# A tuned attention-then-FFN kernel: expert-by-expert FFN order, 1 MB weight loads, a new static order, and a joining copy that steps on its reading side

## Chip, core and metric

The kernel runs on one core of a Trainium2 chip. The metric is device time in microseconds (us), the median of several runs. Every run named here is of the fast state, with a mean granted TensorE clock of 1.00 unless said. A profile is one execution; its span is about 1.8 us shorter than the time. TensorE does the matmuls and transposes and writes them to PSUM, a buffer memory from which ScalarE and VectorE copy them; GpSimd does casts and copies; SyncE issues the transfers (DMA) in one queue. A transfer has landed when all its bytes are there.

## The reference, cut to what matters

```python
# q, k, v: (4, 8, 768, 64) float32; every row sees 8 global and the last 96 local keys
scores = q @ k.T / 8 - slope[h] * dist;  a = softmax(where(keep, scores, -1e9))
x = (a @ v).transpose(0, 2, 1, 3).reshape(3072, 512)
h = maximum(maximum(x @ w1, x @ w2), x @ w3)      # three "experts", 512 x 768 each
out = h @ w_out                                    # 768 x 512
```

The kernel works on 24 tiles of 128 tokens. A tile needs its own keys and those of the tile before it.

## The kernel before

Everything is issued in the order of one string, `SCHEDULE`. Each engine takes its own instructions from it first in, first out. Units are a letter and numbers:

```python
# l/L: load q or k (pair of tiles / one tile)   v: load v   w, o: load weights (all issued by SyncE)
# c/C, W, Q: cast to bf16 (last number: 0 ScalarE, 1 VectorE, 2 GpSimd)
# x/X: q/k transposed by TensorE and copied, X..4: by a DMA transpose;  T likewise for the attention output
# Sn.g: scores of tile n, group g (4 heads) + exp on ScalarE;   Mn.g: mask on VectorE
# (a last 1 in S: the bias is added by TensorE, and there is no mask)
# An.g: values matmuls + normalisation on VectorE;  G, V: copies of the global keys and values;  B, K: biases, masks
# Fc.f.j: FFN up, chunk c (2 or 4 tiles), block of 128 columns f, expert j;   Oc.t: FFN down, copy, store;  E: the last chunk's
SCHEDULE = """ ... S13.0.0 M13.0 L15 L16 v13 v14 S13.1.0 X14.4 F2.5.2 ... """
```

The parts that the change touches:

```python
def u_x(p, a, how):            # a pair of tiles was loaded with even and odd tokens side by side
    ...                        # 8 transposes into tp (PSUM, bf16): [c, e, j, i], e = even/odd
    copies[how % 2](pt[:, a].rearrange("c j (i e) -> c e j i", e=2), tp)      # stepped writes

def u_F1(c, f, j):             # 4 matmuls of 512 (or 256) columns into one of three PSUM buffers
    ...
    if j == 0:   nc.scalar.copy(h01, ps)
    elif j == 1: nc.vector.tensor_max(h01s[c, f], h01s[c, f], ps)
    else:        nc.vector.tensor_max(ht[c][:, f], h01s[c, f], ps)

def load_w(g, j):              # nine loads of 0.5 MB: 256 columns of one expert
    st = stage_pool.tile([128, 4, 256], FP32, name="wst", tag="wst")
    nc.sync.dma_start(out=st, in_=wsrc[j][:, g * 256:(g + 1) * 256].rearrange("(i p) f -> p i f", p=128))
```

The softmax here doesn't subtract the row's maximum and nothing guards it: scores larger than these inputs give would overflow.

## Time and profile before

| | kernel before |
|---|---|
| time, median of 3 | 183.83 us (183.54 to 184.5) |
| span of the profile | 181.9 us |
| TensorE busy | 167.0 us (92%) |
| first matmul / first FFN matmul | 5.69 / 26.27 us |
| last matmul's start to the end | 3.64 us |

The lines behind this table stand in the prediction. One caution: the profile of before lacks 22 of the program's 1528 matmul records. A missing record looks like a gap of two matmuls, 0.43 us from start to start. I count it as two matmuls, not as a wait.

### The profile page before, as it was taken

The page shows a single profiled execution, that of the slowest core. Times are in us where ns is not written, and L with a number is a line of the kernel's source. Part 1 is how long each engine was busy: PE and PEld are TensorE (multiplying, and loading weights), DVE is VectorE, ACT ScalarE, POOL GpSimd, SP SyncE. Part 2 cuts the span into 40 slices and gives each one's busy share as a digit, 9 for nine tenths or more (in the row PEclk, how much of TensorE's full clock was granted, in tenths as well). Part 3 has the DMA queues.
Part 4 walks back from the last instruction along what each step waited for, and adds up shares of the span by engine and source line. Part 5 has one row for each costly group of instructions (what it writes and reads, how often), then busy time and mean ns, then how long its engine had stood idle before and what let it go on. Part 6 is the DMA issues. An engine that isn't in the chain of part 4 may idle for free.

```text
span 181.9 us, 3991 instructions
## 1 busy us (share of the span) xinstructions
PE 167.0 (92%) x1506; PEld 94.3 (52%) x1528; DVE 123.4 (68%) x283; ACT 106.4 (58%) x165; POOL 31.6 (17%) x55
## 2 busy tenths in 40 slices
PE   0587999999999999997999999999999999999992
PEld 0353565567766687763455545445544545544441
DVE  3676477978987578867798758968456995264420
ACT  5968997947789596761437742326735536512222
POOL 6203424203303220212300040222022000000000
PEclk9999999999999999999999999999999999999999
DMA  5999999999998999999987998996799451610006
GB/s 147 271 252 274 294 305 310 306 246 296 267 236 167 226 256 228 261 207 216 193 184 147 272 208 167 241 177 131 200 315 193 90 119 29 231 58 0 4 9 221
DMA packets 93891, 36.18 MB, mean 199 GB/s; under 512 B 77104, under 2 KB 90160, under 8 KB 93872
## 3 DMA queue, kind: packets, MB, share of 16 engines
q1 hardware_dynamic: 93872, 35.92, 88.7%
q8 instruction: 12, 0.20, 0.5%
q14 instruction: 7, 0.06, 0.1%
HBM read 25.17 MB, written 6.29 MB: 173 GB/s over the span
## 4 chain that ended last, share of the span: by engine, by line
PE 71%; DMA 13%; SPq 4%; ACT 4%; DVE 3%; issue 2%; POOL 1%; DVEq 0%; POOLq 0%
PE h L336 41%; PE po L351 17%; DMA rawv<-in_v_dram 6%; PE sp L260 5%; DMA wst<-in_moe_w_dram 4%; SPq L156 3%; DMA rawp<-in_k_dram 3%; PE op L297 3%; PE op L300 2%; ACT P L265 2%; ACT qkT L221 1%; DVE qkT L221 1%; PE xtp L324 1%; PE tp L238 1%; PE tpp L218 1%
## 5 line engine op out<-in xcount | busy, mean ns | idle before, releaser
L336 PE MATMUL h<-xT,w 128*128 128x512 bf16 (+1 forms) x487 | 98.5, 348 | 0.8
L336 PEld LDWEIGHTS <-w 128*128 128x128 bf16 x504 | 47.0, 98 | 39.4
L265 ACT ACTIVATE P<-sp 128x1024 bf16<-128x1024 f32 (+1 forms) x48 | 43.8, 955 | 18.8 <-PE sp L260 18.7
L341 ACT CAST h<-h 128x512 bf16<-128x512 f32 (+1 forms) x42 | 22.1, 529 | 35.6 <-PE h L336 35.2
L343 DVE TENSOR_TENSOR h<-h,h 128x512 bf16<-128x512 bf16 (+1 forms) x42 | 25.5, 607 | 17.7 <-PE h L336 16.7
L351 PE MATMUL po<-wo,ht 128*128 128x512 bf16 (+1 forms) x145 | 33.2, 371 | 0.3
L284 DVE TENSOR_TENSOR P<-P,wmask 128x1024 bf16<-128x1024 bf16 x33 | 22.6, 690 | 11.8 <-ACT P L265 11.5
L345 DVE TENSOR_TENSOR ht<-h,h 128x512 bf16<-128x512 bf16 (+1 forms) x42 | 25.4, 608 | 3.0 <-PE h L336 0.2
L307 DVE TENSOR_TENSOR xb<-op,rz 128x256 bf16<-128x256 f32 x48 | 20.4, 424 | 1.6
L351 PEld LDWEIGHTS <-ht 128*128 128x128 bf16 x150 | 13.8, 98 | 14.2
L357 ACT COPY ost<-po 128x512 f32<-128x512 f32 (+1 forms) x22 | 12.6, 579 | 14.1 <-PE po L351 12.2
L260 PE MATMUL sp<-qkT 64*128 64x128 bf16 x352 | 15.4, 222 | 1.5 <-DVE qkT L221 1.0
L260 PEld LDWEIGHTS <-qkT 64*128 64x128 bf16 x352 | 10.1, 95 | 12.7 <-issue 8.5
L297 PEld LDWEIGHTS <-P 128*128 128x128 bf16 x192 | 13.1, 99 | 5.0 <-ACT P L265 1.7
L297 PE MATMUL op<-va,P 128*128 128x65 bf16 x160 | 13.2, 193 | 2.4 <-POOL va L176 1.1
L306 DVE RECIPROCAL rz<-op 128x4 f32<-128x4 f32 x48 | 8.5, 176 | 8.1 <-PE op L300 6.4
L300 PEld LDWEIGHTS <-P 128*128 128x128 bf16 x160 | 10.6, 97 | 2.9 <-issue 1.3
L218 PE MATMUL tpp<-identb,qkp 128*128 128x128 bf16 x64 | 6.2, 253 | 6.5 <-DVE qkp L170 6.5
L300 PE MATMUL op<-va,P 128*128 128x65 bf16 x128 | 10.6, 193 | 0.0
L400 POOL CAST w<-wst 128x1024 bf16<-128x1024 f32 x5 | 5.7, 1144 | 18.1 <-DMA wst<-in_moe_w_dram 15.0
L176 POOL CAST va<-rawv 128x512 bf16<-128x512 f32 x10 | 6.4, 640 | 12.8 <-DMA rawv<-in_v_dram 12.1
L218 PEld LDWEIGHTS <-qkp 128*128 128x128 bf16 x64 | 4.7, 114 | 6.8 <-DVE qkp L170 6.8
(67 smaller groups left out, 112.1 us busy)
## 6 DMA issues: line engine op xcount, KB each, us to landing
rawv<-in_v_dram SPq DMA_DIRECT2D x24, 256.0 KB, 5.3
out_dram<-ost SPq DMA_DIRECT2D x23, 256.0 KB, 2.9
wst<-in_moe_w_dram SPq DMA_DIRECT2D x9, 512.0 KB, 7.7
raw<-in_q_dram SPq DMA_DIRECT2D x16, 256.0 KB, 4.8
raw<-in_k_dram SPq DMA_DIRECT2D x16, 256.0 KB, 4.9
rawp<-in_q_dram SPq DMA_DIRECT2D x4, 512.0 KB, 6.4
rawp<-in_k_dram SPq DMA_DIRECT2D x4, 512.0 KB, 6.6
wst<-in_moe_w_out_dram SPq DMA_DIRECT2D x3, 512.0 KB, 6.2
```

The costliest lines, as they stand in the source:

```text
L218: nc.tensor.transpose(tp[:, e, jp], qb[p, a][:, e, 2 * jp:2 * jp + 2].rearrange("i h d -> i (h d)"), identb)
L260: nc.tensor.matmul(sp[:, hh, j2, ds], qT(T - ds, 1)[hsl, jp], qT(T, 0)[hsl, jp], start=not how, stop=True, skip_group_check=True)
L265: nc.scalar.activation(P[:, :, 0:n], sp.rearrange("p a b d n -> p (a b) d n")[:, :, 0:n], AF.Exp, bias=0.0, scale=scale)
L284: nc.vector.tensor_mul(P, P, wmask[:, g, :, 0:2])
L297: nc.tensor.matmul(o, P[:, i, 0], heads(va[T])[:, h], start=True, stop=(t == 0), skip_group_check=True)
L300: nc.tensor.matmul(o, P[:, i, 1], heads(va[T - 1])[:, h], start=False, stop=True, skip_group_check=True)
L307: nc.vector.tensor_tensor(out=x[:, 4 * g:4 * g + 4], in0=op[:, :, 0:64], in1=rz[:, :, None].to_broadcast([128, 4, D]), op=ALU.mult)
L336: nc.tensor.matmul(ps, w123[f // 2][:, dm, j, (f % 2) * 128:(f % 2) * 128 + 128], xT[c][:, dm], start=(dm == 0), stop=(dm == 3))
L341: nc.scalar.copy(h01, ps)
L343: nc.vector.tensor_max(h01s[c, f], h01s[c, f], ps)
L345: nc.vector.tensor_max(ht[c][:, f], h01s[c, f], ps)
L351: nc.tensor.matmul(po, ht[c][:, f, tt * 128:(tt + 1) * 128], wo[:, f, cols], start=(f == 0), stop=(f == NF - 1))
```

## The change

The intent: let the FFN start on fewer weights (expert after expert), move the last 512 columns of each expert in one 1 MB load, keep a tile's two score groups together, and make the joining copy cheaper. The core of the diff (the order is rewritten throughout, and with it which engine does a cast or a copy):

```diff
-        copies[how % 2](pt[:, a].rearrange("c j (i e) -> c e j i", e=2), tp)
+        copies[how % 2](pt[:, a].rearrange("c j (i e) -> c j i e", e=2), tp.rearrange("c e j i -> c j i e"))
 ...
-        st = stage_pool.tile([128, 4, 256], FP32, name="wst", tag="wst")
+        n = 256 * (1 + g)
+        st = stage_pool.tile([128, 4, n], FP32, name="wst", tag=f"wst{g}")
 ...
-    ... F0.0.0 M4.0 M4.1 A4.0 A4.1 F0.0.1 ... F0.0.2 F0.1.0 F0.1.1 w1.0 ...
+    ... F0.0.0 V3.1 F0.1.0 F0.0.1 w1.0 F0.1.1 A4.0 A4.1 F0.0.2 F0.1.2 ... F0.2.0 F0.3.0 F0.4.0 ...
 ...
-    ... S13.0.0 M13.0 L15 L16 v13 v14 S13.1.0 ...
+    ... L15 S11.0.0 M11.0 S11.1.0 v13 v14 v15 v16 M11.1 ...
```

More of the change, by code (lines that the diff above doesn't have):

```diff
@@ L25 @@
 SCHEDULE = """
-    B0.1 c0.0.1 B1.2 v0 l1.0 K0 l1.1 v1 K1 K2 B2.0 K3 K4 K5 B3.0 B4.0 B5.0 B6.0 c0.1.1 x0.0.1 x0.1.3
-    B7.0 K6 S0.0.1 c1.0.1 M0.0 S0.1.1 C0.1.2 K7 A0.0 c1.1.1 x1.0.2 M0.1 v2 A0.1 G0.1 S1.0.0 C1.1.0 T0.0
-    S1.1.1 M1.0 A1.0 l2.0 l2.1 M1.1 x1.1.1 G1.2 A1.1 c2.0.0 S2.0.1 M2.0 S2.1.1 M2.1 C2.1.2 v3 G2.0 V1.1
-    A2.0 x2.0.2 A2.1 V2.1 l3.0 c2.1.2 S3.0.1 M3.0 S3.1.1 T1.1 x2.1.0 w0.0 G3.1 C3.1.2 A3.0 c3.0.2 v4
-    M3.1 w0.1 x3.0.2 A3.1 W0.0.2 w0.2 T2.1 S4.0.1 v5 T3.1 C4.1.1 V3.1 l3.1 S4.1.1 W0.1.1 G4.0 F0.0.0
@@ L31 @@
-    M4.0 M4.1 A4.0 A4.1 F0.0.1 S5.0.0 S5.1.0 M5.0 T4.1 M5.1 c3.1.0 W0.2.2 F0.0.2 F0.1.0 F0.1.1 w1.0
-    W1.0.0 V4.2 C5.1.2 A5.0 A5.1 x3.1.0 F0.1.2 F0.2.0 w1.1 w1.2 W1.1.2 T5.1 W1.2.1 S6.0.0 S6.1.0 F0.2.1
-    M6.0 v6 w2.0 F1.0.0 F0.2.2 F0.3.0 F1.0.1 F1.0.2 F1.1.0 L8 M6.1 C6.1.1 F1.1.1 w2.1 G6.2 F0.3.1 W2.1.2
-    W2.0.0 A6.0 A6.1 F1.1.2 C8.0.0 F1.2.0 F0.3.2 S7.0.0 S7.1.0 v7 C7.1.2 v8 F1.2.1 M7.0 w2.2 F1.2.2
-    F1.3.0 o0 M7.1 F0.4.0 X8.3 F1.3.1 o2 A7.0 A7.1 W2.2.2 T6.0 F1.3.2 F1.4.0 C8.1.0 Q0.1 L9 Q2.1 F0.4.1
@@ L36 @@
-    V7.1 L10 G7.2 S8.0.0 S8.1.0 o1 C9.0.0 M8.0 M8.1 F0.4.2 v9 G8.0 F0.5.0 F0.5.1 A8.0 A8.1 v10 X9.0
-    C10.0.0 F1.4.1 Q1.2 F0.5.2 X10.4 T7.0 F1.4.2 S9.0.0 C9.1.0 L11 S9.1.0 T8.1 M9.0 F1.5.0 M9.1 v11 L12
-    O0.0.0 O0.1.0 O0.2.0 V8.1 A9.0 A9.1 T9.4 F1.5.1 C10.1.2 F1.5.2 G9.0 S10.0.0 S10.1.0 O0.3.0 C11.0.3
-    F2.0.0 X11.0 G10.0 C11.1.0 L13 M10.0 M10.1 V9.2 A10.0 v12 F2.0.1 A10.1 V10.1 T10.4 F2.0.2 F2.1.0
-    S11.0.0 S11.1.0 F2.1.1 F2.1.2 M11.0 M11.1 F2.2.0 F2.2.1 F2.2.2 F2.3.0 L14 C12.0.2 X12.0 A11.0 A11.1
@@ L41 @@
-    O1.0.0 S12.0.0 C13.0.1 M12.0 S12.1.0 M12.1 C12.1.2 O1.1.0 X13.0 A12.0 F2.3.1 F2.3.2 C14.0.2 A12.1
-    F2.4.0 F2.4.1 F2.4.2 T11.1 F2.5.0 F2.5.1 G12.1 S13.0.0 M13.0 L15 L16 v13 v14 S13.1.0 X14.4 F2.5.2
-    F3.0.0 F3.0.1 F3.0.2 F3.1.0 M13.1 F3.1.1 C15.0.1 C13.1.2 C14.1.2 C16.0.2 F3.1.2 A13.0 v15 L17 G13.2
-    A13.1 V13.1 X15.4 X16.4 F3.2.0 F3.2.1 F3.2.2 S14.0.0 S14.1.0 M14.0 M14.1 F3.3.0 v16 F3.3.1 F3.3.2
-    T12.4 C17.0.1 A14.0 A14.1 F3.4.0 F3.4.1 T13.4 T14.4 v17 F3.4.2 G14.2 S15.0.0 S15.1.0 M15.0 C15.1.1
@@ L46 @@
-    X17.4 O2.0.0 L18 G15.0 O2.1.0 M15.1 V14.2 A15.0 A15.1 F3.5.0 S16.0.0 v18 S16.1.0 T15.1 G16.1 L19
-    M16.0 F3.5.1 M16.1 V15.2 F3.5.2 C16.1.0 F4.0.0 A16.0 F4.0.1 F4.0.2 A16.1 O3.0.0 S17.0.0 T16.4
-    C18.0.2 M17.0 S17.1.0 V16.1 F4.1.0 C17.1.2 M17.1 F4.1.1 F4.1.2 F4.2.0 F4.2.1 C19.0.1 X18.4 C18.1.2
-    A17.0 A17.1 L20 L21 O3.1.1 X19.4 v19 C20.0.3 F4.2.2 S18.0.0 M18.0 v20 S18.1.0 M18.1 F4.3.0 F4.3.1
-    F4.3.2 F4.4.0 F4.4.1 F4.4.2 F4.5.0 A18.0 A18.1 C21.0.3 F4.5.1 X20.4 X21.4 F4.5.2 T17.4 G18.1 S19.0.0
@@ L51 @@
-    S19.1.0 G19.0 C19.1.2 M19.0 M19.1 T18.4 C20.1.2 O3.2.0 O3.3.0 A19.0 A19.1 T19.4 L22 O4.0.0 S20.0.0
-    M20.0 S20.1.0 O4.1.0 O4.2.0 M20.1 V19.2 A20.0 A20.1 L23 v21 G20.0 F5.0.0 F5.0.1 F5.0.2 F5.1.0 F5.1.1
-    F5.1.2 v22 T20.4 C22.0.3 V20.2 S21.0.0 M21.0 S21.1.0 M21.1 C21.1.1 F5.2.0 X22.4 G21.0 F5.2.1 F5.2.2
-    F5.3.0 A21.0 A21.1 V21.1 F5.3.1 F5.3.2 T21.4 C22.1.0 S22.0.0 S22.1.0 C23.0.3 M22.0 M22.1 F5.4.0
-    F5.4.1 F5.4.2 X23.4 A22.0 A22.1 v23 F5.5.0 G22.1 F5.5.1 F5.5.2 S23.0.0 T22.4 M23.0 V22.2 C23.1.0
@@ L56 @@
-    S23.1.0 M23.1 O4.3.1 O5.0.0 O5.1.0 A23.0 A23.1 O5.2.0 T23.0 O5.3.0 F6.0.0 F6.0.1 F6.0.2 F6.1.0
-    F6.1.1 F6.1.2 F6.2.0 F6.2.1 F6.2.2 F6.3.0 F6.3.1 F6.3.2 F6.4.0 F6.4.1 F6.4.2 F6.5.0 F6.5.1 F6.5.2 E
+    K0 K1 K2 K3 K4 K5 K6 K7 l1.0 v0 v1 B0.1 B1.0 c0.0.1 c0.1.1 B2.1 B3.1 B4.2 B5.0 B6.0 x0.0.2 x0.1.3
+    c1.0.0 S0.0.1 B7.2 S0.1.1 M0.0 M0.1 C0.1.2 C1.1.0 A0.0 G0.0 x1.0.2 A0.1 S1.0.1 S1.1.1 l1.1 M1.0 G1.1
+    l2.0 c1.1.2 l2.1 M1.1 c2.0.1 v2 w0.1 v3 v4 x1.1.2 w0.0 A1.0 A1.1 c2.1.2 V1.2 x2.0.1 C2.1.2 S2.0.1
@@ new lines @@
+    S2.1.1 G2.2 C3.1.2 T0.1 M2.0 M2.1 A2.0 x2.1.2 A2.1 V2.1 S3.0.1 S3.1.1 T1.0 T2.0 G3.2 W0.1.2 M3.0
+    M3.1 A3.0 W0.0.2 A3.1 S4.0.0 T3.1 w0.2 S4.1.0 M4.0 M4.1 G4.1 C4.1.1 W0.2.0 F0.0.0 V3.1 F0.1.0 F0.0.1
+    w1.0 F0.1.1 A4.0 A4.1 F0.0.2 F0.1.2 W2.0.0 S5.0.0 M5.0 l3.0 S5.1.0 M5.1 W1.0.2 F0.2.0 F0.3.0 F0.4.0
+    c3.0.2 x3.0.3 v5 C5.1.2 T4.0 w1.1 V4.2 A5.0 W2.1.0 l3.1 F0.5.0 W1.1.2 c3.1.1 F0.2.1 F0.3.1 x3.1.2
+    A5.1 F0.4.1 w1.2 W1.2.0 F0.5.1 S6.0.0 S6.1.0 v6 C6.1.0 v7 C7.1.0 T5.0 M6.0 M6.1 W2.2.2 F0.2.2 F0.3.2
@@ new lines @@
+    F0.4.2 F0.5.2 F1.0.0 F1.1.0 A6.0 F1.2.0 A6.1 L8 F1.0.1 F1.1.1 o2 Q2.0 G6.0 S7.0.0 o0 S7.1.0 F1.2.1
+    G7.0 F1.0.2 F1.1.2 T6.0 M7.0 M7.1 F1.3.0 F1.4.0 F1.5.0 A7.0 C8.0.2 X8.3 A7.1 Q0.0 v8 o1 L9 L10
+    F1.3.1 F1.4.1 F1.5.1 S8.0.0 S8.1.0 v9 V7.2 G8.1 L11 C8.1.0 M8.0 Q1.2 O0.0.0 v10 v11 C9.0.2 M8.1
+    O0.1.0 A8.0 X9.0 A8.1 V8.2 O0.2.0 C10.0.0 T7.1 F1.2.2 F1.3.2 F1.4.2 S9.0.0 M9.0 S9.1.0 M9.1 C9.1.2
+    L12 L13 L14 G9.1 X10.1 O0.3.0 F2.0.0 F2.0.1 A9.0 F2.1.0 A9.1 F1.5.2 F2.0.2 v12 F2.2.0 T8.1 S10.0.0
@@ new lines @@
+    S10.1.0 F2.1.1 F2.2.1 F2.3.0 C11.0.2 X11.0 M10.0 F2.4.0 M10.1 F2.1.2 F2.5.0 V9.2 G10.1 C10.1.2 A10.0
+    A10.1 V10.2 C11.1.2 C12.0.2 X12.4 C12.1.2 C13.0.0 X13.4 F2.2.2 T9.1 F2.3.1 F2.3.2 L15 S11.0.0 M11.0
+    S11.1.0 v13 v14 v15 v16 M11.1 O1.0.0 F2.4.1 A11.0 O1.1.0 T10.0 A11.1 F2.5.1 F2.4.2 T11.0 S12.0.0
+    M12.0 S12.1.0 G12.1 M12.1 F2.5.2 C14.0.0 F3.0.0 F3.1.0 A12.0 A12.1 F3.0.1 C15.0.1 X14.3 S13.0.0
+    S13.1.0 G13.1 M13.0 M13.1 X15.4 O2.0.0 C13.1.0 F3.0.2 C14.1.1 C15.1.2 F3.2.0 A13.0 A13.1 C16.1.1
@@ new lines @@
+    F3.1.1 F3.2.1 S14.0.0 S14.1.0 G14.2 V13.1 T12.4 M14.0 M14.1 F3.3.0 F3.1.2 F3.4.0 L16 T13.4 A14.0
+    A14.1 F3.3.1 F3.4.1 S15.0.0 S15.1.0 C16.0.3 L17 L18 M15.0 M15.1 F3.5.0 T14.4 O2.1.0 G15.2 V14.2
+    A15.0 X16.1 A15.1 V15.2 T15.4 F3.2.2 F3.3.2 C17.0.0 F3.4.2 S16.0.0 M16.0 S16.1.0 L19 F3.5.1 F3.5.2
+    X17.4 v17 A16.0 M16.1 F4.0.0 F4.1.0 C18.0.3 F4.0.1 F4.1.1 G16.2 v18 C17.1.0 A16.1 F4.0.2 X18.4
+    F4.1.2 S17.0.0 S17.1.0 L20 T16.4 F4.2.0 F4.3.0 F4.4.0 V16.1 C19.0.1 M17.0 X19.4 L21 M17.1 v19 A17.0
@@ new lines @@
+    A17.1 C20.0.3 v20 C18.1.1 O3.0.1 S18.0.0 M18.0 S18.1.0 O3.1.0 C19.1.2 M18.1 F4.2.1 A18.0 A18.1
+    F4.3.1 F4.4.1 G18.1 X20.4 S19.0.0 S19.1.0 C20.1.0 F4.5.0 M19.0 M19.1 T17.4 F4.2.2 O3.2.0 A19.0 A19.1
+    T18.4 F4.5.1 T19.4 L22 V19.2 G19.2 C21.0.3 O3.3.1 S20.0.0 M20.0 S20.1.0 G20.1 X21.4 v21 L23 v22
+    F4.3.2 v23 F4.4.2 A20.0 F4.5.2 M20.1 F5.0.0 F5.0.1 F5.1.0 A20.1 C22.0.1 C23.0.2 F5.0.2 F5.1.1
+    S21.0.0 S21.1.0 F5.2.0 M21.0 M21.1 F5.3.0 F5.2.1 F5.3.1 C21.1.0 C22.1.2 F5.1.2 X22.4 O4.0.0 V20.1
@@ L58 @@
+    A21.0 T20.4 A21.1 F5.2.2 F5.3.2 G21.0 S22.0.0 S22.1.0 M22.0 M22.1 F5.4.0 F5.4.1 X23.4 G22.1 C23.1.0
+    V21.2 A22.0 F5.5.0 A22.1 O4.1.0 F5.5.1 S23.0.0 M23.0 S23.1.0 F5.4.2 M23.1 T21.4 T22.4 O4.2.0 F5.5.2
+    O4.3.0 V22.1 A23.0 A23.1 T23.4 O5.0.0 O5.1.0 O5.2.0 O5.3.1 F6.0.0 F6.1.0 F6.2.0 F6.0.1 F6.1.1 F6.2.1
+    F6.3.0 F6.0.2 F6.1.2 F6.2.2 F6.4.0 F6.5.0 F6.3.1 F6.4.1 F6.3.2 F6.4.2 F6.5.1 F6.5.2 E
 """
@@ L109 @@
     xT_pool = ctx.enter_context(tc.tile_pool(name="xT", bufs=3))
-    stage_pool = ctx.enter_context(tc.tile_pool(name="stage", bufs=12))
+    stage_pool = ctx.enter_context(tc.tile_pool(name="stage", bufs=3))
     ht_pool = ctx.enter_context(tc.tile_pool(name="ht", bufs=2))
@@ L387, in load_w @@
     def load_w(g, j):
-        st = stage_pool.tile([128, 4, 256], FP32, name="wst", tag="wst")
+        n = 256 * (1 + g)
+        st = stage_pool.tile([128, 4, n], FP32, name="wst", tag=f"wst{g}")
         wst[g, j] = st
-        nc.sync.dma_start(out=st, in_=wsrc[j][:, g * 256:(g + 1) * 256].rearrange(
-            "(i p) f -> p i f", p=128))
+        nc.sync.dma_start(out=st, in_=wsrc[j][:, 256 * g:256 * g + n].rearrange("(i p) f -> p i f", p=128))
     def load_wo(i):
-        st = stage_pool.tile([128, 2, DM], FP32, name="wst", tag="wst")
+        st = stage_pool.tile([128, 2, DM], FP32, name="wost", tag="wost")
         wst["o", i] = st
@@ L399, in cast_w @@
     def cast_w(g, j, how):
-        copies[how](w123[g][:, :, j], wst[g, j])
+        src = wst[0, j] if g == 0 else wst[1, j][:, :, 256 * (g - 1):256 * g]
+        copies[how](w123[g][:, :, j], src)
     def cast_wo(i, how):
```

## The prediction

> **What bounds the kernel now.** I read the page first: its busy times, its 40 slices, its chain.
>
> ```profile
> PE 167.0 (92%) x1506; PEld 94.3 (52%) x1528; DVE 123.4 (68%) x283; ACT 106.4 (58%) x165; POOL 31.6 (17%) x55
> PE   0587999999999999997999999999999999999992
> DMA  5999999999998999999987998996799451610006
> PE 71%; DMA 13%; SPq 4%; ACT 4%; DVE 3%; issue 2%; POOL 1%; DVEq 0%; POOLq 0%
> ```
>
> The reader should see that TensorE is full from the seventh slice on, with one hole in the nineteenth, and that the transfers are full for the first 55 us. Matmul ends are modelled, so next I priced TensorE's work from start-to-start times: 0.216 us for a matmul of 512 columns, half of it for 256, 34 ns for a score matmul, 31 ns for one of 65 columns, 55 ns for a transpose. The counts by line then give: FFN up 360 x 0.216 + 144 x 0.108 = 93.4; FFN down 138 x 0.216 + 12 x 0.108 = 31.1; scores 352 x 0.034 = 12.1; bias 14 x 0.216 + 4 x 0.108 = 3.5; attention times values 352 x 0.031 = 10.9; transposes 152 x 0.055 = 8.4. Sum 159.4 us of the 181.9 us span. So 22.5 us are lost, and the rest of the reading is about where. The table of stretches and the timeline of TensorE answer that.
>
> ```profile
> 0.00:7.50 7.50, 1.03 (x8) 0.77 (x8) 2.93 (x16) 5.25 (x12) 3.42 (x13) 1.00 0.82 193
> 28.00:32.00 4.00, 3.95 (x42) 2.05 (x40) 3.00 (x7) 2.88 (x4) 1.77 (x3) 1.00 1.05 314
> 80.00:90.00 10.00, 8.79 (x68) 4.32 (x68) 7.64 (x15) 3.02 (x5) 2.79 (x5) 1.00 1.16 220
> 160.00:173.00 13.00, 12.95 (x61) 5.86 (x61) 6.92 (x11) 2.93 (x5) 0.00 (x0) 1.00 0.01 2
> 178.60:182.00 3.40, 0.00 (x0) 0.00 (x0) 0.42 (x1) 0.00 (x0) 0.00 (x0) 1.00 0.45 158
> ```
>
> ```profile
> 26.27 1.04 PE L336 MATMUL h<-xT,w 128*128 128x512 bf16 x3
> ```
>
> The second column is TensorE's busy time (matmuls). The first matmul starts at 5.69. The first FFN matmul is at 26.27, and of the 26.27 us before it only 11.7 us are priced work, a lag of 14.6 us. From 28 us on there is nearly none, except 1.5 us between 80 and 90, and a tail of 3.4 us (last copy and last store). So a change of order can win only in the first 28 us, at 85 us, or by making the tail shorter. The chain shows what the two holes wait for:
>
> ```profile
> 15.69 7.86 DMA wst<-in_moe_w_dram
> 23.61 1.05 POOL w L400
> ...
> 77.60 1.44 SPq L156
> 79.08 0.88 SPq L156
> 80.01 4.82 DMA rawv<-in_v_dram
> 84.97 0.78 POOL va L176
> 85.79 0.19 PE op L297
> ```
>
> At the start it is the arrival of the first FFN weights behind q, k and v in one queue; at 85 us it is one load of v, which stood in SyncE's order behind stores and q/k loads and was issued too late.
>
> **What the Trainium skill says.** (1) "TensorE: Matmul & The Clock Gate", section "Wait — 56ns, not 53.3ns?", gives N ÷ 2.4 GHz + 2.5 ns from start to start on a warm array: 215.7 ns for 512 columns, and twice that on a cold one. The trace agrees: 216 ns, and 427 ns at 13.6 us, before the clock is granted. No reordering makes the FFN matmuls faster. (2) "VectorE: DVE Perf Modes", section "What auto-detection actually checks": two elements per cycle need 16-bit tensors that all have step ±1. (3) "ScalarE: Activation LUTs", section "What ACT_TABLE_LOAD costs": 186 ns + 0.833 ns per element, so 1039 ns for 1024. (4) "PSUM — Partial Sum Buffer", section "Specifications (TRN2)": 8-byte cachelines, a non-contiguous pattern slows matmuls; of reads by ScalarE or VectorE it says nothing there, and no copy of this trace reads PSUM so. The rows for (2) and (3):
>
> ```profile
> L221 ACT COPY qkT<-tpp 128x1024 bf16<-128x1024 bf16 x5 | 6.5, 1320 | 0.2 <-PE tpp L218 0.2
> L243 ACT COPY qkT<-tp 128x1024 bf16<-128x1024 bf16 x4 | 4.1, 1025 | 0.5 <-PE tp L238 0.4
> L221 DVE COPY qkT<-tpp 128x1024 bf16<-128x1024 bf16 x3 | 3.8, 1300 | 0.0
> L325 DVE COPY xT<-xtp 128x512 bf16<-128x512 bf16 x8 | 3.4, 421 | 2.7 <-PE xtp L324 2.7
> ```
>
> L221 is the copy that joins even and odd tokens, here by stepped writes. ScalarE's plain copy of the same size takes the page's time (1025 against 1039), so stepped writing costs it 0.3 us. VectorE's 421 ns for 512 is two per cycle, the 1300 ns for 1024 one per cycle.
>
> **The change part by part.**
>
> *The joining copy.* Eight copies; the read is stepped now, the write plain. ScalarE should go back to about 1.05 us (five copies x 0.27 = 1.3 us of ScalarE). VectorE still has a stepped tensor, so I keep one per cycle, about 1.2 us. In the new order four of the first six copies lie on ScalarE, on the chain exp - copy - scores - exp that it is full with between 12 and 28 us.
>
> *Weights in 1 MB loads.* Nine loads become six; bytes stay. Rows become 2 KB: in this trace the output weights with 2 KB rows land 1.33 to 1.46 us apart per 0.5 MB, the others 1.42 to 1.60. At 0.1 us for each of six half-megabytes that is an estimated 0.6 us earlier at the end of the weights. Against this, one load lands as a whole: its first 256 columns can be used 1.5 us later than if they came alone.
>
> *FFN order.* With expert after expert, a weight load feeds two or four units of work before the next is needed. The number of matmuls does not change.
>
> *Mixture of the order.* The builds show 16 bias matmuls in place of 18 (-0.43) and 48 transposes of later q/k tiles in place of 40 (+0.44): TensorE's price is again 159.4.
>
> *The start, step by step.* I take landings from the trace: q/k pair loads 1.83 us apart, v 1.16, weights 1.5, and 2.97 for the first weight behind loads of other kind. In the new queue order: second load 6.8 (as now), three more pair loads and v0, v1 to 14.6, l2.1 16.4, v2 17.6, w0.1 20.5, v3 and v4 22.8, w0.0 24.3, w0.2 25.8, w1.0 28.8, then l3.0 and v5 31.7, w1.1 34.7, l3.1 36.5, w1.2 39.4. GpSimd's cast of 1.05 us makes w0.0 usable at 25.4. The other condition is the fourth tile's transposed output: ScalarE's masks and biases end at 8.65, then joining copy 1.05, cast 1.06, two short exps to 11.9, cast 0.6, copy to 13.7, and per tile two exps of 1.03 and a copy of 1.05; the fourth tile's exps end at about 22.7, its normalisation, transpose and copy at 24.5. So the first FFN matmul comes at about 25.4, with 10.8 us of priced work before it: a lag of 14.6 us, just as now. One unit (four matmuls of 512) is 0.86 us, and I walk on with lag 14.6: w1.0 needed at 31.7 and ready at 29.9; w1.1 needed at 36.0, ready at 35.8; w1.2 needed at 40.7, ready at 40.5. Two margins of 0.2 us with landings that I know to about 1 us: I charge 0.5 us.
>
> *The hole at 85 us.* The load that is waited for is the v of tile 13, which was requested between that tile's own two score groups. Now v13 to v16 are requested together at tile 11's scores. I expect this hole (1.2) and two small ones at 88 and 141 us (0.3 and 0.3) to go: -1.7.
>
> *Spacing of scores and values.* Both score groups side by side leave less other work between a tile's scores and its use: often 2.0 us before the first group, 2.8 before the second. The chain needs 1.03 + 0.69 + 0.1 = 1.9 and 1.03 more minus the second group's 0.28 = 2.6. It fits with 0.1 to 0.2 us; I charge 0.2 in all. The tail keeps its form: 0.
>
> Sum: -1.7 + 0.5 + 0.2 = -1.0, so 182.8.
>
> **Rivals.** (a) Stepped reading of PSUM is slow on ScalarE or VectorE, say 2 us a copy. For: the 8-byte cachelines and no example here. Against: one element per cycle already is the slow way on VectorE. The four copies then push the fourth tile by up to 4 us against 0.9 us of slack, and the time becomes about 185.5. (b) The first weight load does not pay the extra 1.5 us, or 2 KB rows are faster than estimated: weights are never waited for, the lag falls by 0.9, and with -1.7 it is about 181.2. (c) The 1 MB loads land as a whole and late, TensorE waits at 36 and 41 us about 1 us each: 183.9, no gain. (d) The loads of v were only the last of several things: a new wait behind SyncE's in-order stores takes the hole's place: about 184.
>
> **Range and chances.** Central 182.5, between the sum (182.8) and the friendlier (b). The pieces that can move are about 1 us each, so 8 in 10 lie in 180.7 to 184.7. Over 2% faster means under 180.2, which needs the lag of the start cut by 2 us besides: 0.08. Over 2% slower, above 187.5, needs (a) at its worst: 0.04. The rest 0.88.
>
> **What would show it.** Right: the hole in the nineteenth slice filled; first FFN matmul at 25 to 26 us with the weights' cast just before it; ScalarE's joining copy near 1.05 us, VectorE's near 1.2; TensorE's busy time unchanged within 1 us. Wrong: joining copies well over 1.3 us, first FFN matmul after 27, waits of TensorE on weights between 30 and 42 us longer than 1 us, a new wait on v or on a transpose by DMA after 60 us, or a first FFN matmul before 24.5, which would make it faster than I say.

## The result and the profile after

| | before | after |
|---|---|---|
| time, median | 184.0 us (4 runs) | 182.22 us (181.75 to 182.46, 4 runs) |
| the same, 5 more rounds | 183.94 us (11 runs) | 182.30 us (6 runs) |
| span of the profile | 181.9 us | 180.0 us; 180.7 in a second profile |
| first FFN matmul | 26.27 us | 24.98; 25.63 in the second |
| last weights of the FFN landed | 46.22 us | 39.05; 38.79 in the second |

The ratio is 0.990 (95% interval 0.9865 to 0.9934), and 0.9905 (0.9887 to 0.9923) in the five more rounds. A ratio is the mean time of one kernel's fast runs over that of the other's in the same rounds, so not quite the ratio of the medians.

The page of the changed kernel: busy times, TensorE's slices, the chain.

```profile
PE 167.2 (93%) x1534; PEld 94.5 (52%) x1534; DVE 122.0 (68%) x282; ACT 108.2 (60%) x164; POOL 35.0 (19%) x59
PE   0589979999999999999999999999999999999993
PE 78%; DMA 9%; SPq 9%; POOL 2%; issue 1%; DVE 0%; DVEq 0%; POOLq 0%
```

The hole in the nineteenth slice is filled, and TensorE's busy time has not moved. The timeline of TensorE alone, with the waits ahead of an instruction in brackets:

```profile
24.98 3.63 PE L336 MATMUL h<-xT,w 128*128 128x512 bf16 x16 [0.35 <-POOL w L402]
...
76.55 0.40 PE L260 MATMUL sp<-qkT 64*128 64x128 bf16 x8 [0.23 <-DMA qkT<-qkb]
...
101.55 3.63 PE L336 MATMUL h<-xT,w 128*128 128x512 bf16 x16 [0.45 <-DMA xT<-xb]
```

The first FFN matmul waits for the cast of its weights, as predicted. After 26 us only two waits are named, and both are new: on DMA transposes. The prediction had named such a wait as a sign of being wrong. The chain of waits at the start:

```profile
16.89 6.95 DMA wst<-in_moe_w_dram
23.89 1.05 POOL w L402
24.98 3.63 PE h L336 x16
```

In the kernel before this was not so, though the prediction reads it so. There the cast of the first weights is done 1.6 us ahead of the first FFN matmul (26.27):

```profile
23.61 1.04 POOL L400 CAST w<-wst 128x1024 bf16<-128x1024 f32 x1 [1.93 <-DMA wst<-in_moe_w_dram]
```

TensorE has no pause above 0.2 us there between 20.4 and 27.4 us. Its pauses lie before, around scores and values, and one of 0.4 us lies at 27.4, behind an exp that stands behind a joining copy on ScalarE.

The stretches with the second column as TensorE's busy time, for comparison with the rows in the prediction:

```profile
28.00:32.00 4.00, 4.00 (x47) 2.16 (x46) 3.45 (x8) 1.79 (x2) 2.19 (x3) 1.00 1.14 312
80.00:90.00 10.00, 10.00 (x100) 5.36 (x99) 9.06 (x22) 6.47 (x10) 0.83 (x2) 1.00 1.32 225
90.00:110.00 20.00, 19.55 (x175) 9.92 (x172) 16.61 (x35) 10.81 (x15) 2.76 (x6) 1.00 1.31 209
```

And the joining copy, one group for each engine:

```profile
L221 ACT COPY qkT<-tpp 128x1024 bf16<-128x1024 bf16 x5 | 5.0, 1009 | 1.5 <-PE tpp L218 1.5
L221 DVE COPY qkT<-tpp 128x1024 bf16<-128x1024 bf16 x3 | 3.7, 1220 | 1.2 <-PE tpp L218 1.2
```

ScalarE's copy fell from 1.32 to 1.01 us, VectorE's from 1.30 to 1.22.

To see where the time came from, I took each matmul's start-to-start time minus the prediction's price for it, and summed the rest by stretch. Missing records are put in by the order of the program, and the prices are scaled to the prediction's 159.4 us in all:

| TensorE's loss, us | before | after | after, second profile |
|---|---|---|---|
| up to the first matmul | 5.69 | 5.84 | 5.71 |
| first matmul to 30 us | 9.52 | 8.38 | 9.16 |
| 30 to 70 | 0.96 | 0.86 | 0.81 |
| 70 to 90 | 1.67 | 0.81 | 0.64 |
| 90 to 120 | 0.42 | 1.15 | 1.33 |
| 120 to the last matmul | 0.78 | 0.29 | 0.47 |
| last matmul's start to the end | 3.64 | 3.39 | 3.37 |

With the mean of the two profiles after: the first two rows -0.7, 30 to 70 us -0.1, 70 to 90 us -0.9, 90 to 120 us +0.8, the last stretch -0.4, tail -0.3. That makes about -1.6, near the measured -1.6 to -1.8. The two profiles after differ by 0.8 us in one row, so a part is known to some 0.4 us.

### The profile page after: what moved, and what is told of

It is laid out like the page before. It is cut to its first block, busy times and chain, and to the rows that moved or that the text cites. A ratio compares the mean times of both kernels' runs of the same rounds, so it can differ in the third digit from the quotient of the medians.

```text
span 180.0 us, 4007 instructions
## 1 busy us (share of the span) xinstructions
PE 167.2 (93%) x1534; PEld 94.5 (52%) x1534; DVE 122.0 (68%) x282; ACT 108.2 (60%) x164; POOL 35.0 (19%) x59
## 4 chain that ended last, share of the span: by engine, by line
PE 78%; DMA 9%; SPq 9%; POOL 2%; issue 1%; DVE 0%; DVEq 0%; POOLq 0%
PE h L336 50%; PE po L351 16%; PE sp L260 5%; SPq L163 4%; DMA wst<-in_moe_w_dram 4%; SPq L148 3%; DMA qkT<-qkb 3%; PE op L297 3%; DMA xT<-xb 2%; PE op L300 2%; PE tp L238 1%; SPq L392 1%; PE xtp L324 1%; POOL w L402 1%; POOL qkb L185 1%
## 5 line engine op out<-in xcount | busy, mean ns | idle before, releaser
L336 PE MATMUL h<-xT,w 128*128 128x512 bf16 (+1 forms) x504 | 101.4, 349 | 0.8 <-DMA xT<-xb 0.4
L336 PEld LDWEIGHTS <-w 128*128 128x128 bf16 x504 | 46.3, 98 | 40.5 <-POOL w L402 0.9
L351 PE MATMUL po<-wo,ht 128*128 128x512 bf16 (+1 forms) x150 | 33.9, 371 | 0.0
L284 DVE TENSOR_TENSOR P<-P,wmask 128x1024 bf16<-128x1024 bf16 x34 | 23.4, 693 | 9.0 <-ACT P L265 8.9
L357 ACT COPY ost<-po 128x512 f32<-128x512 f32 (+1 forms) x21 | 12.0, 577 | 18.4 <-PE po L351 16.0
L307 DVE TENSOR_TENSOR xb<-op,rz 128x256 bf16<-128x256 f32 x48 | 20.4, 424 | 1.7
L297 PEld LDWEIGHTS <-P 128*128 128x128 bf16 x192 | 13.7, 99 | 4.3 <-ACT P L265 1.2
L297 PE MATMUL op<-va,P 128*128 128x65 bf16 x160 | 14.0, 193 | 0.9 <-ACT P L265 0.8
L300 PEld LDWEIGHTS <-P 128*128 128x128 bf16 x160 | 10.8, 97 | 1.5
L300 PE MATMUL op<-va,P 128*128 128x65 bf16 x128 | 11.2, 193 | 0.0
L176 POOL CAST va<-rawv 128x512 bf16<-128x512 f32 x9 | 5.8, 644 | 17.2 <-PE h L336 9.4
L185 POOL CAST qkb<-raw 128x1024 bf16<-128x1024 f32 x5 | 5.2, 1038 | 19.1 <-issue 13.6
L202 POOL COPY va<-vaf 8x260 int32<-8x260 int32 x10 | 4.4, 440 | 22.5 <-PE op L300 22.5
```

The lines of the kernel that those rows point to most:

```text
L284: nc.vector.tensor_mul(P, P, wmask[:, g, :, 0:2])
L297: nc.tensor.matmul(o, P[:, i, 0], heads(va[T])[:, h], start=True, stop=(t == 0), skip_group_check=True)
L300: nc.tensor.matmul(o, P[:, i, 1], heads(va[T - 1])[:, h], start=False, stop=True, skip_group_check=True)
L307: nc.vector.tensor_tensor(out=x[:, 4 * g:4 * g + 4], in0=op[:, :, 0:64], in1=rz[:, :, None].to_broadcast([128, 4, D]), op=ALU.mult)
L336: nc.tensor.matmul(ps, w123[f // 2][:, dm, j, (f % 2) * 128:(f % 2) * 128 + 128], xT[c][:, dm], start=(dm == 0), stop=(dm == 3))
L351: nc.tensor.matmul(po, ht[c][:, f, tt * 128:(tt + 1) * 128], wo[:, f, cols], start=(f == 0), stop=(f == NF - 1))
```

## The experiments

All twelve passed the check against the reference. They ran in three groups; the median of before in them was 183.79, 183.94 and 183.89 us.

### The joining copy alone, on the kernel before

```diff
-        copies[how % 2](pt[:, a].rearrange("c j (i e) -> c e j i", e=2), tp)
+        copies[how % 2](pt[:, a].rearrange("c j (i e) -> c j i e", e=2), tp.rearrange("c e j i -> c j i e"))
```

> The kernel before with one part of the change: the joining copy reads its even and odd tokens stepped and writes plainly. My theory: ScalarE's copies fall from 1.32 to about 1.01 us and VectorE's from 1.30 to 1.22; before 26 us two of ScalarE's copies lie on the chain that sets the first FFN matmul, so it moves from 26.27 to about 25.7 and the time falls by 0.3 to 0.7 us, 183.3 to 183.7. Rival (the copy alone makes the whole gain of the start): minus 0.9 us or more. Rival (TensorE is back to back there anyway): no change.

Measured: 183.85 us, ratio 1.0009 (0.9992 to 1.0027). The expected gain did not come. The first FFN matmul did come earlier, at 25.80. In this profile TensorE then lost 1.3 us at 56 us. The chain of waits there:

```profile
48.96 6.34 DMA raw<-in_k_dram
...
55.38 0.29 ACT qkb L185
55.67 0.67 issue
56.33 0.59 ACT xT L325
56.92 0.04 issue
56.96 0.38 PE xtp L324 x4
```

A load of k landed at 55.30 (54.17 in the profile of before). ScalarE, first in first out, waited with a cast of it, and behind that cast stood the copy that frees the PSUM buffer which TensorE needs. So half a microsecond won at 26 us was lost in this profile to a load that is not any earlier.

### The same with that copy on another engine

```diff
-    ... X10.4 T7.0 F1.4.2 ...
+    ... X10.4 T7.1 F1.4.2 ...
```

> The kernel before with the stepped reading, and the copy of tile 7's transposed output on VectorE in place of ScalarE, where in the run with the stepped reading alone it stood behind a cast that waited for a late load and TensorE lost 1.3 us at 56 us. My theory (the copy's gain at the start was given back there): no hole at 56 us, ratio 0.997 to 0.999. Rival (TensorE gives the gain back elsewhere, or it is not there): ratio 1.000 or above.

Measured: 183.58 us, ratio 0.9984 (0.9967 to 1.0001). That is the expected size, but the interval touches 1, and the hole at 56 us did not close: 0.7 us of it stayed, now behind VectorE's queue. The same k load landed at 54.63 in this profile, and ScalarE's cast of it did not wait; so this run does not prove that the gain is given back there in every execution.

### v requested 29 entries earlier, on the kernel before

```diff
-    ... F2.3.0 L14 C12.0.2 ... L15 L16 v13 v14 S13.1.0 ...
+    ... F2.3.0 L14 v13 v14 C12.0.2 ... L15 L16 S13.1.0 ...
```

> The kernel before with the loads of v for tiles 13 and 14 requested right after the q and k of tile 14, some 20 us earlier; nothing else. My theory: the 1.2 us hole of TensorE at 85 us closes and nothing takes its place, minus 1.0 to 1.4 us, about 182.7. Rival (a new wait behind SyncE's in-order issues takes its place): within 0.3 us of the kernel before.

Measured: 183.05 us, ratio 0.996 (0.9939 to 0.9981), so -0.7 us, less than expected. The hole at 85 us is gone; a smaller one of 0.4 us shows at 88 us. The load was not issued some 20 us earlier but 6.7 (at 73.34 in place of 80.01): SyncE issued it right behind tile 14's k (72.72).

### Both together

```diff
 # the edits of the joining copy and of v13 v14 above, together
```

> The kernel before with the stepped reading and the early loads of v together. If the two are the gain and simply add, minus 1.4 to 2.0 us, as fast as the changed kernel (182.2). If the order of the FFN, the weight loads or the new order of the start carry part of it, it stays 0.5 us or more behind the changed kernel.

Measured: 182.51 us, ratio 0.9933 (0.9904 to 0.9962). Between the two expectations. With v mended the joining copy seems to bring something (0.996 to 0.9933), and some 0.3% seems left to the changed kernel (0.9905). The intervals overlap, so neither step is shown; by the middle values they are about 0.5 us each. In this profile the k load landed at 53.99, there is no hole at 56 us, and the first FFN matmul is at 26.09.

### The changed kernel with the old joining copy

```diff
-        copies[how % 2](pt[:, a].rearrange("c j (i e) -> c j i e", e=2), tp.rearrange("c e j i -> c j i e"))
+        copies[how % 2](pt[:, a].rearrange("c j (i e) -> c e j i", e=2), tp)
```

> The changed kernel with the old joining copy, stepped writing. My theory: the first FFN matmul waits for the cast of its weights, which ends at 24.94, only 0.2 us after the transposed output of the fourth tile; three of ScalarE's copies of 0.3 us each lie on the way to that output, so it comes about 0.6 us later and the time rises by 0.4 to 0.9 us, 182.6 to 183.1. Rival (the weights hide it): no change, 182.2. Rival (the copy carries the whole start): plus 1 us or more.

Measured: 182.39 us, ratio 0.9929 (0.9911 to 0.9948), against 0.9905 (0.9887 to 0.9923) for the changed kernel in other rounds: +0.24%, about 0.4 us. The intervals overlap, so this is not shown, and the reason I gave did not hold. TensorE's timeline:

```profile
25.46 3.63 PE L336 MATMUL h<-xT,w 128*128 128x512 bf16 x15 [0.77 <-POOL w L402]
```

The first FFN matmul still waits for the cast, and comes between the 24.98 and 25.63 of the changed kernel's two profiles. So in this order the weights hide the joining copy at the start. In the kernel before they do not: the three profiles with the stepped reading have the first FFN matmul at 25.80, 25.87 and 26.09, the others at 26.25, 26.27 and 26.75, and the pause at 27.4 us is gone in the three.

### The changed kernel again

```diff
 # no edit
```

> The changed kernel itself, unaltered, in the same rounds as the three next. All theories: its ratio to the kernel before stays at 0.990 (0.9865 to 0.9934); its trace shows the first FFN matmul at 25.0 and two holes of TensorE at about 76 and 101 us of 0.3 to 0.7 us, if these are of the order and not of chance.

Measured: 182.30 us, ratio 0.9905. The first FFN matmul is at 25.63, not at 25.0: it moves with the landing of its weights (24.48 in place of 23.83). The hole at 101 us is there again (0.66 us), so it belongs to the order. The one at 76 us is not in this profile, but it is in the next one (0.64 us).

### The changed kernel with v requested late

```diff
-    ... S11.1.0 v13 v14 v15 v16 M11.1 ... S13.0.0 S13.1.0 ...
+    ... S11.1.0 M11.1 ... S13.0.0 v13 v14 v15 v16 S13.1.0 ...
```

> The changed kernel with the loads of v for tiles 13 to 16 requested where the kernel before has those of 13 and 14, between tile 13's two score groups. My theory (the request's place makes the hole): a hole before tile 13's values of 1 to 2 us comes back and the time rises by 0.9 to 2 us. Rival (the hole of the kernel before came from its stores and loads ahead in SyncE's order, which this order does not have there): no hole, no change.

Measured: 182.30 us, ratio 0.9904 (0.9884 to 0.9925). No change, and no hole before tile 13's values. My theory, and the prediction's reason, fell: it is not the unit at which v is requested. SyncE's issues in the two kernels, in the timeline of its queue (start, duration, what), first before and then this run:

```profile
75.92 0.39 SPq L156 DMA_DIRECT2D raw<-in_q_dram  x1
76.37 1.18 SPq L156 DMA_DIRECT2D raw<-in_k_dram  x1
77.60 1.44 SPq L156 DMA_DIRECT2D raw<-in_q_dram  x1
79.08 0.88 SPq L156 DMA_DIRECT2D raw<-in_k_dram  x1
80.01 2.09 SPq L163 DMA_DIRECT2D rawv<-in_v_dram  x2
```

```profile
76.98 1.33 SPq L358 DMA_DIRECT2D out_dram<-ost  x2
78.36 4.30 SPq L163 DMA_DIRECT2D rawv<-in_v_dram  x4
```

In the kernel before, v stands behind the q and k loads of two tiles that are not needed until later. Here only two stores are ahead of it: v of tile 13 lands at 83.06 in place of 84.82, and tile 13's values begin at 84.98 without a wait. The edit moved less than it seems to: the unaltered changed kernel, which requests this load two tiles earlier, issues it at 76.25, only 2.1 us before this run.

### Four entries exchanged in the kernel before

```diff
-    ... S13.0.0 M13.0 L15 L16 v13 v14 S13.1.0 ...
+    ... S13.0.0 M13.0 v13 v14 L15 L16 S13.1.0 ...
```

> The kernel before with four entries of its order exchanged: the loads of v for tiles 13 and 14 stand in front of the q and k loads of tiles 15 and 16 and not behind them. My theory after the last runs (the hole came from standing behind four loads in SyncE's order, not from being requested at tile 13): v of tile 13 is issued at about 76 in place of 80.0 and lands about 81, the hole at 85 us is gone, and the time falls as with the loads 20 us earlier, by 0.5 to 1.2 us, ratio 0.994 to 0.997. Rival (it must be requested a tile or more ahead): a hole of 0.5 us or more stays and the time falls by less than 0.3 us.

Measured: 182.91 us, ratio 0.9949 (0.9925 to 0.9972), about -0.9 us, as much as asking farther ahead within the noise. v of tile 13 was issued at 76.23 and landed at 80.27. The stretch from 70 to 90 us, TensorE's busy time in the second column, first before and then this run:

```profile
70.00:90.00 20.00, 18.69 (x185) 11.55 (x186) 15.36 (x36) 9.40 (x15) 4.44 (x7) 1.00 1.15 228
```

```profile
70.00:90.00 20.00, 20.00 (x195) 12.27 (x193) 15.50 (x38) 10.43 (x17) 4.62 (x7) 1.00 1.19 223
```

Closing this hole is the largest single part of the change's gain, and an exchange of two pairs of loads is enough for it.

### The 1 MB loads as two halves each

```diff
-        nc.sync.dma_start(out=st, in_=wsrc[j][:, 256 * g:256 * g + n].rearrange("(i p) f -> p i f", p=128))
+        for gg in ((0,), (1, 2))[g]:       # a tile and a load of 256 columns each
+            nc.sync.dma_start(out=st, in_=wsrc[j][:, 256 * gg:256 * gg + 256].rearrange("(i p) f -> p i f", p=128))
```

> The changed kernel with each 1 MB load of weights made as two loads of 0.5 MB of 256 columns, one after the other in the same place of the queue. My theory: the loads are not what the gain rests on; the second half lands within 0.3 us of where the 1 MB load lands and the time is within 0.3 us of the changed kernel. Rival (rows of 2 KB are worth it): the weights end 0.6 us later and TensorE waits for them, plus 0.5 us. Rival (the halves come earlier, which helps): minus 0.3 us.

Measured: 182.54 us, ratio 0.9927 (0.9904 to 0.995), against 0.9905 (0.9887 to 0.9923) in the same rounds. The intervals overlap, so a cost is not settled. My expectation of the landings was wrong: the last half landed at 40.54, the 1 MB load at 38.79 in the same rounds. The rows of 2 KB are worth about what the prediction estimated: the 1 MB loads follow the load ahead of them by 2.73 to 2.81 us, 1.4 per 0.5 MB, four of the six halves by 1.50 to 1.57, so some 0.7 us in all (estimated from these). The rest comes from one half that landed 2.28 us after the one ahead of it, at 35.47, and from the k load behind it; I have no reason for that. TensorE did not wait for these weights; the profile has one extra gap of 0.26 us at 38 us, ahead of the transposes of a k load that lands 1.5 us later too.

### The old FFN order in chunks 2 to 6, in the same slots

```diff
-    ... F4.0.0 F4.1.0 ... F4.0.1 F4.1.1 A16.1 F4.0.2 F4.1.2 ...
+    ... F4.0.0 F4.0.1 ... F4.0.2 F4.1.0 A16.1 F4.1.1 F4.1.2 ...      # so in every chunk from 2 on
```

> The changed kernel with the FFN of its chunks 2 to 6 in the old order, the three experts of one block of columns after another, in the same slots. My theory: TensorE has no wait there in either order, so within 0.3 us of the changed kernel. Rival (runs of the same expert keep ScalarE and VectorE from taking turns, and the order is part of the gain): plus 0.5 us or more, seen as holes before FFN matmuls after 60 us.

Measured: 187.75 us, ratio 1.0198 (1.0176 to 1.022). Slower than both kernels, far outside my theory; the rival has the direction. The largest loss is a gap of 3.2 us from one matmul's start to the next, at 111.55 us. The timeline of this kernel there (start, busy time, what; the bracket is idle time before it):

```profile
109.05 1.94 ACT L265 ACTIVATE P<-sp 128x1024 bf16<-128x1024 f32 x2 [0.25 <-PE sp L260]
...
110.87 0.59 ACT L341 CAST h<-h 128x512 bf16<-128x512 f32 x1
111.50 0.69 DVE L343 TENSOR_TENSOR h<-h,h 128x512 bf16<-128x512 bf16 x1 [2.09 <-ACT h L341]
112.29 0.69 DVE L345 TENSOR_TENSOR ht<-h,h 128x512 bf16<-128x512 bf16 x1
...
113.41 0.67 DVE L185 CAST qkb<-raw 128x1024 bf16<-128x1024 f32 x1
114.01 1.28 DVE L284 TENSOR_TENSOR P<-P,wmask 128x1024 bf16<-128x1024 bf16 x2
```

A first expert's matmuls fall right behind a tile's scores. Their copy waits on ScalarE behind two exps of about 1 us. VectorE idles for 2.1 us because its next instruction, the second expert's maximum, needs that copy, and the two masks stand behind it. So the values matmuls wait until 114.74. The pause also cost clock (0.50 from 115 to 118 us). The stretch of 100 to 120 us, in which the last but two columns are the granted clock, the transfers' share and GB/s:

```profile
100.00:120.00 20.00, 17.08 (x130) 8.02 (x131) 13.98 (x29) 7.72 (x11) 0.82 (x2) 0.91 0.93 167
```

Values matmuls after it run 50 to 60 ns apart in place of 30. This does not say that the expert order is better as such: the kernel before runs the old order without such holes, in slots that were laid for it. It says that FFN order and slots are one thing.

### The old FFN order in the first chunk

```diff
-    ... F0.2.0 F0.3.0 F0.4.0 ... F0.5.0 F0.2.1 F0.3.1 ...
+    ... F0.2.0 W1.1.2 F0.2.1 W1.2.2 F0.2.2 ... F0.3.0 F0.3.1 F0.3.2 ...
```

> The changed kernel with the FFN of the first chunk, from its third block of columns on, in the old order, all three experts of a block before the next block; the order of the loads in the queue is kept, the casts of the weights are placed before their first use. My theory (expert after expert is what makes the 1 MB loads usable, since a load feeds four units of 0.86 us): TensorE waits at about 32 us for the second expert's load (cast ends 35.6) and at 36 for the third's (cast ends 40.1), together 5 to 7 us, time 187 to 189. Rival (the order of the FFN does not matter at the start because the transfers are the bound in any order): within 1 us.

Measured: 191.67 us, ratio 1.0413 (1.0382 to 1.0443). The direction and the waits are as expected, the cost is above what I gave (187 to 189). TensorE's timeline:

```profile
35.44 1.04 PE L336 MATMUL h<-xT,w 128*128 128x512 bf16 x4 [2.53 <-POOL w L402]
39.94 1.89 PE L336 MATMUL h<-xT,w 128*128 128x512 bf16 x4 [3.46 <-POOL w L402]
```

The two waits are where the landings put them (35.6 and 40.1 expected). From 28 to 42 us the granted clock was 0.84, and the four matmuls after the second pause took 1.89 us in place of 1.04; that part I had not counted. (The edit also moves the casts of the weights and puts the load requests together, in the same order.) With loads of one expert's 512 columns, a block cannot be finished before three loads have landed; expert after expert each load feeds four units.

### A mend of the two new holes

```diff
-    ... V10.2 C11.1.2 C12.0.2 X12.4 ... A15.1 V15.2 T15.4 ...
+    ... C12.0.2 X12.4 V10.2 C11.1.2 ... A15.1 V15.2 T15.1 ...
```

> The changed kernel with its two new holes mended: tile 15's output transposed by TensorE (copy on VectorE) in place of a DMA transpose that TensorE waited for at 101 us; tile 12's q/k cast put in front of two other operations on GpSimd, so that its DMA transpose starts about 1 us earlier. My theory: the 0.6 us hole at 101 us goes for 0.22 us of transposes, the one at 76 us goes where it showed; 0.3 to 0.8 us faster than the changed kernel, ratio to before about 0.987. Rival (the earlier TensorE only waits for the next thing): no change, 0.990.

Measured: 182.89 us, ratio 0.9944 (0.9929 to 0.996), slower than the changed kernel. The mend failed. TensorE's timeline:

```profile
96.76 0.27 PE L324 MATMUL xtp<-identb,xb 128*128 128x128 bf16 x2 [0.64 <-DVE qkT L243]
97.31 0.28 PE L324 MATMUL xtp<-identb,xb 128*128 128x128 bf16 x2 [0.28 <-DVE xb L307]
```

I put the transposes where the DMA transpose was issued, right behind the tile's values. A DMA waits there beside TensorE; TensorE's own transposes wait in its queue, first for a PSUM buffer and then for the normalisation, 1.2 us in all. The hole at 101 us closed and a larger one opened at 97. There is no hole at 76 us in this profile, but that one comes and goes. Two FFN units later would be the place to try; that was not run. No run here beats the changed kernel.

## Why the prediction was right, point by point

**The time.** 182.5 us predicted, 182.2 to 182.3 measured, inside 180.7 to 184.7, and neither 2% faster nor 2% slower, to which it gave 0.88. Part of that is luck: the charge for weights (0.5) did not come and the start and the tail brought 0.9 that was not counted, while the waits after 90 us cost 0.6 more than charged and the holes gave 0.4 less. The price of TensorE's work has two slips: with the printed prices FFN up is 93.3 and the scores 12.0, so 159.1 in all; nothing hangs on it.

**What bounds the kernel.** Held: busy time 167.0 and 167.2, and nearly all that was won or lost lies in the first 28 us, at 85 us, in new waits and a little in the tail.

**The joining copy.** Its duration held: 1.05 and 1.2 us predicted, 1.01 and 1.22 measured. Rival (a), slow stepped reads of PSUM, is out. What it is worth in time is not shown: in the new order it is off the path at the start, and on the kernel before alone it brought nothing clear of noise.

**The start.** First FFN matmul predicted at 25.4 behind the weights' cast: 24.98 and 25.63, behind that cast. First weights predicted to land at 24.3: 23.83 and 24.48. The later ones (28.8, 34.7, 39.4) landed at 28.27, 34.57 and 39.05. The lag of 14.6 us held within 0.4 for the new kernel: 14.2 and 14.9 at the first FFN matmul. "Just as now" was a coincidence: the prediction says that the kernel before waits for these weights, but there they were cast at 24.65, 1.6 us ahead of their use. And the kernel before lost a further 0.4 us at 27.4 us, just behind its first FFN matmul, which I left out. So this term is about -0.7 in place of 0.

**The charge of 0.5 us for weights at 36 and 41 us.** Wrong: none of the profiles of the changed kernel shows such a wait. Rival (c) is out.

**The hole at 85 us.** The size held roughly: -1.7 predicted with the two small ones; -0.9 between 70 and 90 us and -0.4 after 120 us in the traces, while v alone, in the kernel before, brought 0.7 to 0.9 us. The reason failed: "requested at tile 11's scores" is not needed. What counts is not standing behind the loads of two later tiles.

**The spacing of scores and values, 0.2 us.** Mis-sized, with another cause. The scores and values did not wait for each other; TensorE waits for two DMA transposes, which with the rest of 90 to 120 us costs about 0.8 us. Rival (d) named such a wait, behind SyncE's stores; of its guess only the half is right, as the xT transpose is issued on time (97.12) and takes 4.4 us.

**The tail, 0.** It is 0.25 us shorter (3.64 to 3.39 and 3.37). The last store ends sooner; with the halved loads it was 3.62 again. I have no explanation, and no run was made for it.

**What stays open.** Whether the kernel before with copy and v mended (0.9933) is behind the changed kernel (0.9905) at all, as the intervals overlap; and if by some 0.5 us, how that divides among the load order, the 1 MB loads and the expert order. The runs show that these belong together (each old order in the new slots costs 5.4 to 9.4 us against the changed kernel), not what each is worth in an order laid for it.

## What to carry to other kernels

In a queue that issues in order, ask what stands ahead of the load that is needed next: exchanging it with loads for later tiles brought about 0.9 us (0.5 to 1.4), where the whole change brought 1.7. A static order on in-order engines cannot be judged by its parts: the same matmuls in the other order in the same slots cost 5 to 9 us, because an instruction that waits holds back those behind it. When one engine is full, price its work first; then only the few stretches where it starves can gain, and a microsecond won ahead of a full transfer queue may be taken back at the next load.

## What the Trainium skill lacked or had wrong

- "PSUM — Partial Sum Buffer", section "Specifications (TRN2)": its remark on non-contiguous patterns is for matmuls only. No page has a figure for a copy by ScalarE that steps through PSUM. Here one that takes its bf16 elements in turn from two places 1 KB apart pays nothing: 1.01 us for 1024 elements, 1.025 for the plain copy. VectorE's takes 1.22 (0.68 for a plain one, in the mended run), its stepped writing 1.30.
- "SBUF — State Buffer" (the memory that the casts and copies write), the note on SBUF cachelines (in the section "Door 1: The DMA port swizzle (why `[64,N]` ≈ `[32,N]`)") lets bf16 be stepped by up to 8 elements for free. ScalarE's copy with writes stepped by 2 elements took 1.32 us, against 1.01 when the same copy steps on the PSUM side.
- "TensorE: Matmul & The Clock Gate", section "What's actually happening", gives the cold state after at least one idle window of about 3.4 us. A pause of 2.8 us (3.2 from one matmul's start to the next) was enough in the run with the old order in chunks 2 to 6: the granted clock was 0.50 from 115 to 118 us just after it, and values matmuls ran 50 to 60 ns apart in place of 30.
- "DMA: Bandwidth & Descriptors", section "Specifications": line rate from 512 B on. In the kernel before, loads of 0.5 MB landed 1.71 to 1.85 us behind the load ahead of them with rows of 512 B (q and k of the start) and, but for the first (2.97), 1.42 to 1.60 with rows of 1 KB; in the changed kernel it is 1.36 to 1.41 per 0.5 MB with rows of 2 KB.
